# Top-k attention, a gated MLP and routed experts in one kernel: where three pieces of the expert weights' conversion stand beside the routing of the last tokens

## The chip, the cores and the metric

The kernel runs on one core of one Trainium2 chip. A core has TensorE (matrix products), VectorE, ScalarE and GpSimd (elementwise work and reductions) and SyncE, which here only issues transfers; in the profile they are PE, DVE, ACT, POOL and SP. Transfers of every issuer are carried by 16 DMA engines. Each engine runs its own list of instructions in order and waits for others by semaphores. The metric is the device time of one execution in microseconds (us); lower is better.

## What is computed

Three stages, each fed by the one ahead of it. The reference, cut to its core:

```python
scores = scale * np.matmul(q, k.transpose(0, 1, 3, 2))          # 2 x 8 heads, 576 x 576
kth = np.partition(scores, -32, axis=-1)[..., -32:-31]
attn = softmax(np.where(scores >= kth, scores, -1e9))
x = np.matmul(attn, v)                                          # 1152 tokens x 512
xn = x / np.sqrt(np.mean(x * x, -1) + 1e-6) * rms_g
y = (silu(xn @ w_gate) * (xn @ w_val)) @ w_out                  # 512 -> 1536 -> 512
logits = y @ r_gate                                             # 8 experts, each token goes to its best one
# each expert takes its first 288 tokens, in their order
h = np.maximum(np.einsum('ecd,edf->ecf', disp, w1), 0.0)        # 512 -> 1024
out[i] = gate_w[i] * np.einsum('ecf,efd->ecd', h, w2)[expert_idx[i], pos[i]]
```

## The kernel before, in words

The 1152 tokens are nine tiles of 128, t = 0 to 8. Attention runs by head pair and tile; behind it, interleaved by hand-written slots (`at`, `advance`), run `norm(t)`, `moe1(t)` (the dense MLP of a tile) and `dispatch(t)` (its routing). A scheduler replays the traced instructions on a timeline of its own and so sets each engine's list. A block written under `tc.issue_after(ins)` is put in the list of the engine of `ins` behind `ins`; on other engines it has no effect. It orders and adds no semaphore.

**The routing of a tile** (L486 to L570): TensorE transposes the MLP's output `yx` (L490), ScalarE copies it to `xu` (L492) and sums the squares (L497), TensorE makes the logits (L503, eight small matmuls), VectorE copies them (L506) and takes the maximum (L526), GpSimd negates it (L529), ScalarE takes the exponentials `ex` (L531). VectorE makes `key`, `k8` and the one-hot `oh` (L533, L536, L539). TensorE counts the tokens ahead (L542, L543; L541 in tile 8 alone). VectorE makes the position of each token (L547 to L555) and its `slot` (L563), and GpSimd scatters the rows to `disp` in DRAM (L565). The MLP of the last tiles stands beside this: `hT` transposed by TensorE (L436) and copied (L422, L423), the product with `w_out` (L475) and `yx` (L481).

**The weights of the experts** are 16 matrices of 2 MB, counted here by n, their place in the load order `ORDER` (n = 0, 1 are expert 0's up and down, 2, 3 expert 1's, and 4 expert 2's up). SP loads each in two halves (L718). `size` (L723) sums its squares (ScalarE L731, into a scratch `junk`; VectorE L734; TensorE L736 adds over partitions) and finds a power of two by six small VectorE operations (L737 to L742 and the helpers L139, L142). `convert` (L749) writes the fp16 high part `hi` (L756 on ScalarE, L758 on VectorE) and the low part `lo` (L761 on VectorE). Raw matrices 2 and 3 have a buffer each; 4 is loaded into that of 2 when 2 has been split, and 5 into that of 3.

**The experts.** Expert 0 runs in two parts. Part "a" is its first 128 rows: the ones that tiles 0 to 7 have filled, so the gather "a" (a transposing DMA on ScalarE's queue, `xgT`, L772) and its `notes` (L785) are traced in tile 8's routing and wait for tile 7's scatter. Part "b" is the rest, 48 rows, gathered behind tile 8's scatter by GpSimd (`xb`, L828) and turned by SP (`xbT`, L832). The products (L845) are 96 matmuls each: up a, down a, up b, down b, up 1, then up e and down e - 1 for e = 2 to 7. An up product is evicted to `hE` (ScalarE L855, VectorE L856), a down product to `yT2` (L864); `send` transposes that (L883), scales it to `ob` (L885) and scatters it to the output (L887). Between them `ready()` (L904) does the `size` of matrix n + 1, the `convert` of n and the load of a later one, from n = 4 on.

The lines around the change are those behind the dense MLP, where `size` and `convert` of the first matrices are traced. In the kernel before, matrix 3 stands under `tc.issue_after(scat[-1].ins)`, an instruction of GpSimd, on which neither `size` nor `convert` has any instruction.

Of the kernel before, what the change touches and what calls it, by code (L numbers as in the profile page):

```python
# [1 line left out]

# [12 lines left out]
AF = mybir.ActivationFunctionType  # L15
OP = mybir.AluOpType
# [9 lines left out]
NT = N // P  # L26
# [19 lines left out]
def tile_topk_attention__then__moe__then__moe_routed(  # L46
# [3 lines left out]
    nc = tc.nc  # L50
# [79 lines left out]
    def pow2_below_rsqrt(out, back, x, by, t):  # L130

        nc.gpsimd.tensor_scalar(t[:, 0:1], x, by, TINY, op0=OP.mult, op1=OP.add)
        nc.gpsimd.tensor_tensor(t[:, 1:2], t[:, 0:1], mhalf, op=OP.pow)
        yield
        exponent(out, t[:, 1:2])
        invert(back, out)

    def exponent(out, x):
        nc.vector.tensor_scalar(out.bitcast(I32), x.bitcast(I32), 0x7f800000, None, op0=OP.bitwise_and)  # L139

    def invert(out, x):
        nc.vector.tensor_scalar(out.bitcast(I32), x.bitcast(I32), -1, 0x7f000000, op0=OP.mult, op1=OP.add)  # L142
# [338 lines left out]
        nc.scalar.activation(yx[t], yps, AF.Copy, scale=ydec)  # L481
        yield

    scat = []

    def dispatch(t):  # L486
        y = yx.pop(t)
# [10 lines left out]
        size = iter(()) if t == NT - 1 else pow2_below_rsqrt(yn[:, 1:2], yn[:, 2:3], yn[:, 0:1], 1.01, yn[:, 3:5])  # L498
# [6 lines left out]
        lg = route.tile([P, E], F32, name="lg")  # L505
# [22 lines left out]
        nm = route.tile([P, 4], F32, name="nm")  # L528
        nc.gpsimd.tensor_scalar(nm[:, 0:1], m8[:, 0:1], -1.0, None, op0=OP.mult)  # L529
        ex = route.tile([P, E], F32, name="ex", bufs=1)  # L530
        nc.scalar.activation(ex, lg, AF.Exp, bias=nm[:, 0:1], accum_out=nm[:, 1:2])  # L531
        key = route.tile([P, E], F32, name="key", bufs=1)
        nc.vector.scalar_tensor_tensor(key, lg, m8[:, 0:1], rank8, op0=OP.is_ge, op1=OP.mult)  # L533
        yield
# [10 lines left out]
        pos = route.tile([P, 4], F32, name="pos")  # L545
# [14 lines left out]
            gather("a", 0, 0, WA, ew, nc.scalar)  # L560
            notes("a", 0, 0, WA, ew, nc.scalar)
        slot = route.tile([P, 1], I32, name="slot")
        nc.vector.tensor_tensor(slot, pos[:, 3:4], pos[:, 2:3], op=OP.add)  # L563
        nc.gpsimd.tensor_tensor(cum, cum, oh, op=OP.add)
        scat.append(nc.gpsimd.indirect_dma_start(  # L565
            out=disp, out_offset=bass.IndirectOffsetOnAxis(ap=slot[:, :1], axis=0),
# [73 lines left out]
    for p in range(NP):  # L640
        t, hp = divmod(p, 4)
# [12 lines left out]
    for t in range(NT):  # L654
        ew = nc.vector if t in (0, 8) else nc.gpsimd
        t0 = (4 * t + 5) * SL
        at(t0 + 1, ahead(norm(t, ew), 300), 1)
        at(t0 + (12 if t < NT - 1 else 18), ahead(moe1(t, ew), 0), 2.7)
        at(t0 + 10 + 4 * SL, ahead(dispatch(t), 0), 3 if t < NT - 1 else 1)
    live = []  # L660
    slot = 0
# [30 lines left out]
    ORDER = [0, 1, 2, 3, 4]  # L692
# [9 lines left out]
    def place(j):  # L702
        x = slots[slot_of[j]].bitcast(F16)
        return x[:, :8 * DM], x[:, 8 * DM:]

    def raw_of(n):

        if n < 2:
            return slots[2 + n]
        return raws[n % 2 if n < 4 else n % 4]  # L710
# [12 lines left out]
    def size(j, n):  # L723

        e, w = divmod(j, 2)
        raw = raw_of(n)
        sc = ew.tile([P, 13], F32, name="sc", bufs=8)
        k = 4 if n < 4 else 2
        for g in range(k):
            junk = ew.tile([P, BIG], BF16, name="junk")[:, :2 * BIG // k]  # L730
            nc.scalar.activation(junk, raw[:, g * 2 * BIG // k:(g + 1) * 2 * BIG // k], AF.Square, accum_out=sc[:, 9 + g:10 + g])  # L731
        t = pst.tile([P, DM], F32, name="st")
        s16 = ew.tile([P, 4], BF16, name="s16", bufs=2)
        nc.vector.tensor_copy(s16[:, :k], sc[:, 9:9 + k])  # L734
        for g in range(k):
            nc.tensor.matmul(t[:, 0:1], ones16, s16[:, g:g + 1], start=(g == 0), stop=(g == k - 1))  # L736
        nc.vector.tensor_scalar(sc[:, 2:3], t[:, 0:1], 1.01, TINY, op0=OP.mult, op1=OP.add)  # L737
        half_bits = sc[:, 3:4].bitcast(I32)
        nc.vector.tensor_scalar(half_bits, sc[:, 2:3].bitcast(I32), 1, 0x7fff0000, op0=OP.logical_shift_right, op1=OP.bitwise_and)
        nc.vector.tensor_scalar(half_bits, half_bits, -1, 0x5f370000 + ((10, 14)[w] << 23), op0=OP.mult, op1=OP.add)  # L740
        exponent(sc[:, 7:8], sc[:, 3:4])
        invert(sc[:, 4:5], sc[:, 7:8])  # L742
        if w == 0:
            es[e] = sc
        else:
            nc.vector.tensor_tensor(es[e][:, 8:9], es[e][:, 4:5], sc[:, 4:5], op=OP.mult)
        sized[j] = sc

    def convert(j, n):  # L749

        raw, (hi, lo), sc = raw_of(n), place(j), sized.pop(j)
        k = 4 if n < 4 else 2
        for g in range(k):
            r = slice(g * 2 * BIG // k, (g + 1) * 2 * BIG // k)
            if 2 * g < k:
                nc.scalar.activation(hi[:, r], raw[:, r], AF.Copy, scale=sc[:, 7:8])  # L756
            else:
                nc.vector.tensor_scalar(hi[:, r], raw[:, r], sc[:, 7:8], None, op0=OP.mult)  # L758
        for g in range(k):
            r = slice(g * 2 * BIG // k, (g + 1) * 2 * BIG // k)  # L760
            nc.vector.scalar_tensor_tensor(lo[:, r], raw[:, r], sc[:, 7:8], hi[:, r], op0=OP.mult, op1=OP.subtract)  # L761
# [31 lines left out]
    def fetch_w():  # L793
        n = loaded[0]
        loaded[0] += 1
        if n < 2 * E:
            load(ORDER[n], n)
# [11 lines left out]
    convert(0, 0)  # L809
    size(2, 2)  # L810
    convert(1, 1)
    convert(2, 2)
    fetch_w()
    with tc.issue_after(scat[-1].ins):
        size(3, 3)
        convert(3, 3)
    pacc = ctx.enter_context(tc.tile_pool(name="pacc", bufs=3, space=PSUM, reuse_waits="tile"))
    pback = ctx.enter_context(tc.tile_pool(name="pback", bufs=2, space=PSUM, reuse_waits="tile"))
# [85 lines left out]
    def ready():  # L904

        n = done[0]
        done[0] += 1
        if n >= 2 * E:
            return
        if n == 4:  # L910
            size(ORDER[4], 4)
        if n + 1 < 2 * E:
            size(ORDER[n + 1], n + 1)
        convert(ORDER[n], n)
        fetch_w()

    down("a", 0, WA)
    up("b", 0, WB)
    ready()
    send("a", WA, True)  # L920
    up(1, 1, W)
    ready()
    down("b", 0, WB)
    ready()
    cnt = pback.tile([P, DM], F32, name="back")
    nc.tensor.matmul(cnt[:, :E], ones16, cum, start=True, stop=True)
# [82 lines left out]
```

## Time and profile before

| | |
|---|---|
| three timed runs | 710.47, 708.5, 710.53 us; median 710.47 |
| the profiled execution | 708.96 us, of which the span of the trace is 707.2 |
| busy, share of the span | TensorE 79%, its weight loads 57%, VectorE 89%, ScalarE 70%, GpSimd 59% |
| chain that ended last | VectorE 49%, issue 16%, TensorE 11%, ScalarE 8%, DMA 8%, GpSimd 6% |
| mean granted TensorE clock | 0.935 |

VectorE searches the top 32 of attention up to 497 us; the last product of the dense MLP ends at about 558 us (L475 of tile 8, from 555.50 for 2.33), and the experts follow to the end of the span. A row of a timeline gives start, duration, engine, line, operation, what it writes and reads, and in brackets how long the engine stood idle just before and what released it. The chain is a backward walk from the last instruction. In a row with xN, N instructions lie behind one another and the duration is that of all. The clock is a share of full speed.

### The profile page before, as it was taken

How to read it: one execution, taken by the hardware profiler on the slowest of the kernel's cores; microseconds unless marked ns; L12 is line 12 of the kernel's file. 1: busy time of each engine (PE TensorE's matmuls, PEld its weight loads, DVE VectorE, ACT ScalarE, POOL GpSimd, SP SyncE). 2: the span in 40 equal slices, each digit the busy share in tenths (PEclk: the TensorE clock that was granted, in tenths of full speed). 3: DMA queues.
4: the chain of work that ended last, by engine and by line, in shares of the span. 5: the costliest groups of instructions: out<-in, count | busy, mean ns of one | idle time of the engine just before them, and what ended most of it. 6: DMA issues, size and time to landing. Idle time of an engine off the chain costs nothing.

```text
span 707.2 us, 13015 instructions
## 1 busy us (share of the span) xinstructions
PE 555.5 (79%) x4708; PEld 401.9 (57%) x4708; DVE 627.0 (89%) x1311; ACT 495.8 (70%) x959; POOL 414.9 (59%) x444
## 2 busy tenths in 40 slices
PE   1207424567667999999999999998999489989995
PEld 1106324435344666666656666664645289989994
DVE  3999999999999999999999999999348855999960
ACT  3446537558957879868878797876799537988921
POOL 2786887877696887966767778566631110022312
PEclk9999555679999999999999999999999889999998
DMA  8898171375000001000000000000570449999201
GB/s 244 236 331 282 39 233 38 126 225 188 15 8 8 16 31 43 16 31 10 16 23 16 24 16 24 1 1 16 205 286 1 148 82 382 328 322 347 106 21 38
DMA packets 47016, 80.00 MB, mean 113 GB/s; under 512 B 18732, under 2 KB 23340, under 8 KB 46946
## 3 DMA queue, kind: packets, MB, share of 16 engines
q1 hardware_dynamic: 43954, 74.02, 33.2%
q0 software_dynamic: 1792, 4.83, 1.9%
q8 instruction: 39, 0.64, 0.4%
q10 hardware_dynamic: 1200, 0.26, 0.2%
q14 instruction: 31, 0.25, 0.1%
HBM read 64.35 MB, written 12.27 MB: 108 GB/s over the span
## 4 chain that ended last, share of the span: by engine, by line
DVE 49%; issue 16%; PE 11%; ACT 8%; DMA 8%; POOL 6%; SPq 1%; POOLq 0%; ACTq 0%; DVEq 0%
DVE r L333 14%; DVE m L336 14%; DVE m L324 5%; PE pm L450 4%; DMA wbig<-in_w_out_dram 3%; DVE wbig L157 3%; ACT junk L731 3%; DMA raw<-in_w_dram 3%; POOL out_dram L887 2%; DVE wbig L159 2%; DVE split L761 2%; DVE wbig L228 2%; DMA vt<-in_v_l_dram 2%; PE pm L475 2%; DVE hT L423 1%
## 5 line engine op out<-in xcount | busy, mean ns | idle before, releaser
L450 PE MATMUL pm<-wbig,xn 128*128 128x512 f16 x600 | 152.1, 387 | 8.8 <-POOL wbig L225 3.2
L336 DVE MAX8 m<-r 128x8 f32<-128x576 f32 x216 | 156.8, 745 | 0.3
L845 PEld LDWEIGHTS <-split 128*128 128x128 f16 x1728 | 115.6, 99 | 6.9 <-DMA xbT<-xb 2.5
L310 PE MATMUL tp<-kst,qh 128*128 128x288 f32 (+1 forms) x160 | 65.2, 418 | 63.5 <-ACT s L312 24.2
L353 POOL TENSOR_TENSOR pp<-s,pp 128x576 f32<-128x576 f32 x72 | 102.8, 1442 | 8.6 <-ACT pp L352 8.4
L333 DVE MATCH_REPLACE8 r<-m,r 128x576 f32<-128x576 f32 x144 | 106.3, 740 | 0.0
L450 PEld LDWEIGHTS <-xn 128*128 128x128 f16 x648 | 62.4, 100 | 71.9 <-issue 11.3
L475 PE MATMUL pm<-wbig,hT 128*128 128x512 f16 x324 | 79.1, 383 | 7.7 <-POOL wbig L229 3.7
L310 PEld LDWEIGHTS tp<-kst,qh 128*128 128x128 f32 (+1 forms) x160 | 32.6, 205 | 89.9 <-ACT s L312 32.7
L376 PE MATMUL tp<-ident,pp 128*128 128x128 f32 x324 | 58.7, 298 | 16.1 <-ACT pp L358 7.5
L352 ACT ACTIVATE pp<-s,bias 128x576 f32<-128x576 f32 x72 | 52.0, 773 | 26.4 <-POOL bias L338 26.2
L312 ACT ACTIVATE s<-tp 128x288 f32<-128x288 f32 x144 | 54.8, 412 | 19.2 <-POOL pp L353 15.8
L761 DVE SCALAR_TENSOR_TENSOR split<-raw,sc,split 128x2048 f16<-128x2048 f32 (+1 forms) x32 | 65.8, 2078 | 0.1
L887 POOL DMA_INDIRECT out_dram<-ob,tos x14 | 20.2, 1445 | 73.8 <-ACT ob L885 58.4
L845 PE MATMUL acc<-hE,split 128*128 128x168 f16 (+2 forms) x864 | 58.8, 228 | 3.4 <-ACT junk L731 1.4
L731 ACT ACTIVATE junk<-raw 128x2048 bf16<-128x2048 f32 (+1 forms) x32 | 54.2, 1693 | 9.9 <-DMA raw<-in_w_dram 9.5
L384 PE MATMUL xps<-pt,vt 128*64 128x128 f32 (+1 forms) x800 | 57.8, 284 | 2.9 <-ACT pt L377 2.9
L376 PEld LDWEIGHTS tp<-ident,pp 128*128 128x128 f32 x324 | 42.5, 152 | 31.0 <-ACT pp L358 10.3
L377 ACT ACTIVATE pt<-tp 128x384 f32<-128x384 f32 x108 | 49.3, 494 | 14.9 <-PE tp L376 12.3
L845 PE MATMUL acc<-xgT,split 128*128 128x168 f16 (+1 forms) x768 | 58.0, 239 | 0.0
L358 ACT ACTIVATE pp<-pp,bias 128x576 f32<-128x576 f32 x72 | 56.4, 785 | 0.1
L324 DVE MAX8 m<-s 128x8 f32<-128x576 f32 x72 | 53.6, 745 | 0.0
(198 smaller groups left out, 1233.4 us busy)
## 6 DMA issues: line engine op xcount, KB each, us to landing
raw<-in_w_dram SPq DMA_DIRECT2D x28, 1024.0 KB, 10.2
wbig<-in_w_out_dram SPq DMA_DIRECT2D x6, 1024.0 KB, 8.1
disp<-wraw SPq DMA_DIRECT2D x18, 257.0 KB, 5.5
qraw<-in_q_l_dram SPq DMA_DIRECT2D x72, 64.0 KB, 2.2
wraw<-in_w_gate_dram SPq DMA_DIRECT2D x8, 512.0 KB, 4.5
split<-in_w_dram SPq DMA_DIRECT2D x4, 1024.0 KB, 5.8
kraw<-in_k_l_dram SPq DMA_DIRECT2D x12, 288.0 KB, 4.4
wbig<-in_w_val_dram SPq DMA_DIRECT2D x3, 1024.0 KB, 7.4
```

The source lines that it names most:

```text
L310: nc.tensor.matmul(sp[:c1], x[:, i, :c1], kst[b, hp][:, i, c * HALF:(c + 1) * HALF], start=(n == 0), stop=(n == 1))
L324: nc.vector.max(m[:, i, 0], s[i])
L333: nc.vector.match_replace(r[i], m[:, i, n - 1], src, -3.0e38)
L336: nc.vector.max(m[:, i, n], r[i])
L353: nc.gpsimd.tensor_tensor(w, s[i], w, op=OP.subtract)
L376: nc.tensor.transpose(tp[:, i, :], p2[:, o:o + P], ident)
L384: nc.tensor.matmul(xps[t][rows, hp, c0:c1], v, w, start=(n == 0), stop=(n == 4))
L450: nc.tensor.matmul(a, xn[:, x + c, :], half(i, lo), start=(c == 0 and n == 0), stop=(c == KC - 1 and n == 2))
L475: nc.tensor.matmul(yps, hT[f // KC][:, KC * hi + f % KC, :], half(i, lo), start=(f == 0 and n == 0), stop=(f == NF1 - 1 and n == 2))
L731: nc.scalar.activation(junk, raw[:, g * 2 * BIG // k:(g + 1) * 2 * BIG // k], AF.Square, accum_out=sc[:, 9 + g:10 + g])
L761: nc.vector.scalar_tensor_tensor(lo[:, r], raw[:, r], sc[:, 7:8], hi[:, r], op0=OP.mult, op1=OP.subtract)
L845: nc.tensor.matmul(a, u[:, c, col * P:(col + 1) * P], v[:, c, :a.shape[-1]], start=(c == 0 and n == 0), stop=(c == nk - 1 and n == 2))
```

## The change

Three pieces are put elsewhere, and no arithmetic changes. `dispatch` keeps the instruction `ex` (ScalarE) and `slot` (VectorE) of each tile, and a helper `after(t, ...)` opens `issue_after` on the ones named. The split of matrix 2 now stands behind those of tile 7 (NT - 2), the split of matrix 3 behind those of tile 8 (NT - 1), while the sizing of 3 stands free; the squares of matrix 4 stand behind `ex` of tile 8 on ScalarE.

```diff
--- before.py
+++ after.py
@@ -1,4 +1,4 @@
-from contextlib import ExitStack
+from contextlib import ExitStack, contextmanager
 
 import concourse.bass as bass
 import concourse.tile as tile
@@ -481,7 +481,15 @@
         nc.scalar.activation(yx[t], yps, AF.Copy, scale=ydec)
         yield
 
-    scat = []
+    scat, behind = [], {}
+
+    @contextmanager
+    def after(t, *engines):
+
+        with ExitStack() as stack:
+            for e in engines:
+                stack.enter_context(tc.issue_after(behind[t, e].ins))
+            yield
 
     def dispatch(t):
         y = yx.pop(t)
@@ -528,7 +536,7 @@
         nm = route.tile([P, 4], F32, name="nm")
         nc.gpsimd.tensor_scalar(nm[:, 0:1], m8[:, 0:1], -1.0, None, op0=OP.mult)
         ex = route.tile([P, E], F32, name="ex", bufs=1)
-        nc.scalar.activation(ex, lg, AF.Exp, bias=nm[:, 0:1], accum_out=nm[:, 1:2])
+        behind[t, "act"] = nc.scalar.activation(ex, lg, AF.Exp, bias=nm[:, 0:1], accum_out=nm[:, 1:2])
         key = route.tile([P, E], F32, name="key", bufs=1)
         nc.vector.scalar_tensor_tensor(key, lg, m8[:, 0:1], rank8, op0=OP.is_ge, op1=OP.mult)
         yield
@@ -560,7 +568,7 @@
             gather("a", 0, 0, WA, ew, nc.scalar)
             notes("a", 0, 0, WA, ew, nc.scalar)
         slot = route.tile([P, 1], I32, name="slot")
-        nc.vector.tensor_tensor(slot, pos[:, 3:4], pos[:, 2:3], op=OP.add)
+        behind[t, "dve"] = nc.vector.tensor_tensor(slot, pos[:, 3:4], pos[:, 2:3], op=OP.add)
         nc.gpsimd.tensor_tensor(cum, cum, oh, op=OP.add)
         scat.append(nc.gpsimd.indirect_dma_start(
             out=disp, out_offset=bass.IndirectOffsetOnAxis(ap=slot[:, :1], axis=0),
@@ -809,10 +817,11 @@
     convert(0, 0)
     size(2, 2)
     convert(1, 1)
-    convert(2, 2)
+    with after(NT - 2, "act", "dve"):
+        convert(2, 2)
     fetch_w()
-    with tc.issue_after(scat[-1].ins):
-        size(3, 3)
+    size(3, 3)
+    with after(NT - 1, "act", "dve"):
         convert(3, 3)
     pacc = ctx.enter_context(tc.tile_pool(name="pacc", bufs=3, space=PSUM, reuse_waits="tile"))
     pback = ctx.enter_context(tc.tile_pool(name="pback", bufs=2, space=PSUM, reuse_waits="tile"))
@@ -908,7 +917,8 @@
         if n >= 2 * E:
             return
         if n == 4:
-            size(ORDER[4], 4)
+            with after(NT - 1, "act"):
+                size(ORDER[4], 4)
         if n + 1 < 2 * E:
             size(ORDER[n + 1], n + 1)
         convert(ORDER[n], n)
```

All lines from L484 on are 8 further down in the new file (L563 becomes L571), those from about L845 on 9.

On VectorE, at tile 7's routing, the kernel before has this order (`split_5636` is matrix 2, `split_5637` matrix 3):

```order
L758 TENSOR_SCALAR split_5636<-raw_5638,sc 128x1024
L533 SCALAR_TENSOR_TENSOR key<-lg,m_5661,rank_72 128x8
L758 TENSOR_SCALAR split_5636<-raw_5638,sc 128x1024
L737 TENSOR_SCALAR sc<-st 128x1
L761 SCALAR_TENSOR_TENSOR split_5636<-raw_5638,sc,split_5636 128x1024
L536 MAX k_5684<-key 128x8
L761 SCALAR_TENSOR_TENSOR split_5636<-raw_5638,sc,split_5636 128x1024 x2
L739 TENSOR_SCALAR sc<-sc 128x1
L761 SCALAR_TENSOR_TENSOR split_5636<-raw_5638,sc,split_5636 128x1024
L548 TENSOR_SCALAR nm<-nm 128x1
L539 TENSOR_SCALAR oh<-rank_72,k_5684 128x8
L423 TENSOR_TENSOR hT<-pm,hT 128x512
```

The kernel after has, from the position's last steps to the first instruction of tile 8's chain:

```order
L558 SCALAR_TENSOR_TENSOR scr,pos<-px,oh 128x8
L561 TENSOR_SCALAR pos<-pos 128x1
L562 TENSOR_TENSOR pos<-pos 128x1
L571 TENSOR_TENSOR slot<-pos 128x1
L766 TENSOR_SCALAR split_5636<-raw_5638,sc 128x1024
L423 TENSOR_TENSOR hT<-pm,hT 128x512
L766 TENSOR_SCALAR split_5636<-raw_5638,sc 128x1024
L769 SCALAR_TENSOR_TENSOR split_5636<-raw_5638,sc,split_5636 128x1024 x4
L881 CAST to_6405<-notes_5889 128x1
L518 TENSOR_SCALAR yn<-yn 128x1
```

The six large operations of matrix 2 moved from between the steps of tile 7's routing to behind its slot; those of matrix 3 are no longer in this stretch. Tile 8's slot is followed by them.

On ScalarE, at the routing of tile 8, before (`junk,sc<-raw_5638` are the squares of matrix 4):

```order
L422 ACTIVATE hT<-pm 128x512
L756 ACTIVATE split_5637<-raw_5639,sc 128x1024 x2
L481 ACTIVATE yx<-pm,st 128x512
L731 ACTIVATE junk,sc<-raw_5638 128x2048
L492 ACTIVATE xu<-px 128x512
L772 DMA_TRANSPOSE xgT<-disp 128x8x128
L785 DMA notes_5889<-disp 128x2
L497 ACTIVATE yd,yn<-yx 128x512
L731 ACTIVATE junk,sc<-raw_5638 128x2048
L518 ACTIVATE yd<-yx,yn 128x512
L531 ACTIVATE ex,nm<-lg,nm 128x8
```

and after:

```order
L422 ACTIVATE hT<-pm 128x512
L780 DMA_TRANSPOSE xgT<-disp 128x8x128
L481 ACTIVATE yx<-pm,st 128x512
L793 DMA notes_5889<-disp 128x2
L505 ACTIVATE yd,yn<-yx 128x512
L500 ACTIVATE xu<-px 128x512
L526 ACTIVATE yd<-yx,yn 128x512
L539 ACTIVATE ex,nm<-lg,nm 128x8
L764 ACTIVATE split_5637<-raw_5639,sc 128x1024 x2
L864 ACTIVATE hE_6036<-acc 128x512
```

The squares of 4 and the split of 3 left the stretch ahead of `ex`, and the gather "a" moved ahead of `yx`. Further on, both squares of matrix 5 now stand ahead of the eviction of up b and of the split of 4, where they stood behind them.

On TensorE, at the sum of the squares of matrix 5 (`s_6383`), before:

```order
L845 LDWEIGHTS split_5635
L845 MATMUL acc<-hE_6262,split_5635 128x48
L736 LDWEIGHTS ones_70
L736 MATMUL st<-s_6383,ones_70 128x1
L736 LDWEIGHTS ones_70
L736 MATMUL st<-s_6383,ones_70 128x1
L845 LDWEIGHTS split_5635
L845 MATMUL acc<-hE_6261,split_5635 128x48
```

and after:

```order
L854 LDWEIGHTS split_5636
L854 MATMUL acc<-xgT,split_5636 128x168
L744 LDWEIGHTS ones_70
L744 MATMUL st<-s_6383,ones_70 128x1
L744 LDWEIGHTS ones_70
L744 MATMUL st<-s_6383,ones_70 128x1
L854 LDWEIGHTS split_5636
L854 MATMUL acc<-xgT,split_5636 128x168
```

The sum moved from behind the first 8 matmuls of down b to the middle of up 1, with 49 of its matmuls and all of down b behind it. Ahead of that, in tile 8's routing, L503 stood ahead of every product of up a; now 33 of them stand ahead of it, 25 more ahead of L541, 28 more ahead of L542, and 10 behind. Before, 22 stood between L503 and L541, 9 more ahead of L542, and 65 behind. In tile 7's, L542 and L543 stood behind the first two L475 and now stand ahead of them.

## Rows read from the trace of the kernel before

**Rows 1.** Timeline of VectorE around the routing of tiles 6 (508 us), 7 (548 us) and 8 (to 570.15).

```profile
508.00 0.17 DVE L526 MAX8 m<-lg 128x8 f32<-128x8 f32 x1
...
508.67 0.23 DVE L539 TENSOR_SCALAR oh<-rank,k 128x8 bf16<-128x8 f32 x1
...
547.95 0.17 DVE L526 MAX8 m<-lg 128x8 f32<-128x8 f32 x1
...
554.63 0.22 DVE L539 TENSOR_SCALAR oh<-rank,k 128x8 bf16<-128x8 f32 x1
...
556.03 1.41 DVE L758 TENSOR_SCALAR split<-raw,sc 128x1024 f16<-128x1024 f32 x2
557.35 0.15 DVE L563 TENSOR_TENSOR slot<-pos 128x1 int32<-128x1 f32 x1
...
557.49 4.87 DVE L761 SCALAR_TENSOR_TENSOR split<-raw,sc,split 128x1024 f16<-128x1024 f32 x4
...
570.15 0.15 DVE L563 TENSOR_TENSOR slot<-pos 128x1 int32<-128x1 f32 x1
```

**Rows 2.** Timeline of GpSimd, 558 to 575 us: the scatters of tiles 7 and 8 (L565) and the first instruction behind each that waited for its landing (L495 and L828).

```profile
558.30 1.43 POOL L565 DMA_INDIRECT disp<-yd,slot  x1 [2.92 <-DVE sc L746]
562.60 0.18 POOL L495 COPY yd<-tok 128x1 f32<-128x1 f32 x1 [2.86 <-DMA disp<-yd,slot]
...
571.17 1.06 POOL L565 DMA_INDIRECT disp<-yd,slot  x1 [1.19 <-DVE slot L563]
574.26 0.97 POOL L828 DMA_INDIRECT xb<-disp,rest  x1 [2.03 <-DMA disp<-yd,slot]
```

**Rows 3.** Timeline of ScalarE, 557 to 593 us; ACTq is its queue issuing a transfer.

```profile
557.93 0.67 ACT L481 ACTIVATE yx<-pm,st 128x512 f32<-128x512 f32 x1
...
562.56 1.36 ACTq L772 DMA_TRANSPOSE xgT<-disp  x1
...
563.76 0.58 ACT L492 ACTIVATE xu<-px 128x512 f32<-128x512 f32 x1
...
588.14 1.91 ACT L731 ACTIVATE junk<-raw 128x2048 bf16<-128x2048 f32 x1 [2.60 <-DMA raw<-in_w_dram]
...
591.63 1.91 ACT L731 ACTIVATE junk<-raw 128x2048 bf16<-128x2048 f32 x1 [0.43 <-DMA raw<-in_w_dram]
```

**Rows 4.** Timeline of TensorE, 545 to 603 us, and its four longest waits behind that.

```profile
545.48 0.95 PE L503 MATMUL px<-rg,xu 128*128 128x8 f32 x8
...
551.14 0.60 PE L436 MATMUL pm<-ident,gs 128*128 128x128 f32 x4
...
555.50 2.33 PE L475 MATMUL pm<-wbig,hT 128*128 128x512 f16 x10 [0.41 <-DVE sc L740]
...
564.39 1.88 PE L503 MATMUL px<-rg,xu 128*128 128x8 f32 x8 [5.08 <-ACT xu L492]
566.12 2.51 PE L845 MATMUL acc<-xgT,split 128*128 128x128 f16 x22
...
569.40 0.21 PE L542 MATMUL px<-oh,before 128*128 128x8 bf16 x1
...
575.33 4.79 PE L845 MATMUL acc<-hE,split 128*128 128x128 f16 x83 [0.51 <-DVE hE L856]
582.43 2.60 PE L845 MATMUL acc<-xbT,split 128*128 128x48 f16 x96 [2.30 <-DMA xbT<-xb]
...
593.89 0.19 PE L736 MATMUL st<-s,ones 128*128 128x1 bf16 x2 [1.27 <-DVE s L734]
593.94 2.38 PE L845 MATMUL acc<-hE,split 128*128 128x48 f16 x88
...
596.19 7.12 PE L845 MATMUL acc<-xgT,split 128*128 128x168 f16 x96
...
620.12 2.19 PE L845 MATMUL acc<-hE,split 128*128 128x168 f16 x28 [1.43 <-ACT junk L731]
...
636.26 1.47 PE L845 MATMUL acc<-hE,split 128*128 128x168 f16 x18 [1.09 <-ACT hE L855]
...
667.04 0.19 PE L736 MATMUL st<-s,ones 128*128 128x1 bf16 x2 [0.69 <-DVE s L734]
667.62 7.12 PE L845 MATMUL acc<-hE,split 128*128 128x168 f16 x96 [0.39 <-DVE hE L856]
```

**Rows 5.** The chain of waits in order of time, 545 to 600 us: start, duration, what.

```profile
554.68 7.15 DMA raw<-in_w_dram
...
566.26 2.36 PE acc L845 x22
...
583.51 10.72 DMA raw<-in_w_dram
```

**Rows 6.** Busy time by stretch: the stretch and its length; busy time and (count) of TensorE, its weight loads, VectorE, ScalarE and GpSimd; TensorE's granted clock; the DMA share; GB/s.

```profile
553.00:560.00 7.00, 3.21 (x17) 1.41 (x15) 7.00 (x24) 2.76 (x3) 1.64 (x2) 1.00 0.74 259
560.00:561.00 1.00, 0.00 (x0) 0.00 (x0) 1.00 (x1) 0.00 (x0) 0.00 (x0) 0.80 0.98 398
561.00:570.00 9.00, 5.61 (x48) 5.61 (x49) 4.78 (x26) 6.09 (x10) 0.64 (x3) 0.50 0.20 49
570.00:571.00 1.00, 1.00 (x13) 1.00 (x12) 0.30 (x4) 0.00 (x0) 0.00 (x0) 0.58 0.02 8
603.00:660.00 57.00, 54.49 (x745) 53.71 (x743) 53.69 (x90) 51.09 (x55) 13.02 (x7) 1.00 1.07 325
```

## The prediction

> **What bounds the kernel now.** I read the chain of waits first, then each engine's timeline where the dense MLP ends and the routed experts begin (547 to 604 us), then the clock and the DMA share there. Three things are to be seen.
>
> First, the routing of the last two token tiles is what the experts wait for, and for tile 7 it stands in a row with weight splits on VectorE. In tile 6 the one-hot `oh` starts 0.67 us after the maximum of the logits (508.00 to 508.67); in tile 7 it takes 6.68 us (547.95 to 554.63), and the slot comes at 557.35 [rows 1]. The scatter of tile 7 is issued at 558.30, GpSimd sees it landed at 562.60, and the gather of the first 128 rows (`xgT` "a", L772 on ScalarE's queue) starts at 562.56 [rows 2, 3].
>
> Second, ScalarE's squares of matrix 4 wait for a load that takes 7.15 us from 554.68, and `xu` of tile 8 stands behind these squares and the gather, at 563.76; TensorE waits 5.08 us for it and only then runs tile 8's logits (L503) and the first expert's products [rows 3 to 5]. In the 9 us from 561 TensorE's granted clock is 0.50 of full, its level of 1.2 GHz; it is 0.58 in the next and 1.00, 2.4 GHz, in the later ones [rows 6].
>
> Third, behind tile 8's slot (570.15) the chain goes on through its scatter (571.17), the gather of the rest (574.26) and the load of matrix 5 (from 583.51); ScalarE squares the halves of 5 at 588.14 and 591.63, and TensorE stops 1.27 us, to 593.89, for the sum of these squares [rows 1 to 5]. From 603 to 660 VectorE is busy 53.7 of 57 us, ScalarE 51.1, TensorE 54.5, and the DMA share is full [rows 6]. What is late at 603 has little room to be made up.
>
> **Tile 7's routing (gain).** With the splits of matrix 2 behind the slot, `oh` comes 0.67 after 547.95, plus some small operations: about 548.7. The position matmuls (L542, L543) stand behind four transposes L436, which end at 551.14 + 0.60 = 551.74 [rows 4]; they, not VectorE, now set the position, and the slot follows at about 552.3 (0.75 us from L542 to the slot in tile 8, 569.40 to 570.15 [rows 1, 4], less what runs together). That is 5.0 us before 557.35. The scatter was issued 0.95 after the slot's start in tile 7 and 1.02 in tile 8, and was seen landed 4.30 and 3.09 us later (558.30 to 562.60; 571.17 to 574.26) [rows 1, 2]. Landing after: 552.3 + 0.9 + 3.1 to 4.3, 556.3 to 557.5. I take 556.3: the load of matrix 4, beside which the longer one ran [rows 5], can't start before the splits of 2 have read its buffer, at about 557. The landing comes 6.3 us earlier.
>
> **ScalarE (mixed).** Its order now has the gather "a" ahead of `yx` (L481). `yx` could start at about 556.1, when the last ten L475 (2.33 us [rows 4]) end, behind `hT` at 553.8 (the slot, 0.15, one L758 of 0.7 [rows 1], and a last step about as long), but the engine waits for tile 7's landing and issues for 1.36 us [rows 3]: `yx` at 557.7 against 557.93. Some 1.6 us of a possible 1.8 are given up. But the squares of 4 no longer stand ahead of `xu`: `yx` takes 0.67 us, the notes' issue and L497 I put at as much each, and `xu` comes at 559.7 against 563.76 [rows 3].
>
> The gather lands at most 3.6 us after its issue starts (562.56, to the first products at 566.12 to 566.26 [rows 3, 5]): 556.3 + 3.6 = 559.9. It ran beside little; now the load of 4 begins a microsecond behind it. The nearest row for that is the scatter, 1.2 us longer beside a load, the upper bound; the lower one is below nothing by a little, since 3.6 also holds TensorE's own wait for L503. I take nothing: most of the gather lies ahead of the load.
>
> The Trainium skill, "DMA: Bandwidth & Descriptors", section "Issuing engines are not separate DMA queues", says that transfers issued by ScalarE, SP or GpSimd end on the same 16 engines and interleave. It speaks against the change, which moves the load of 4 from beside the scatter to beside the gather. The two scatters agree, 4.30 us beside the load and 3.09 without. By that rule tile 8's slot would come up to 1.2 us later than in my sum; the sum doesn't use it.
>
> **TensorE up to tile 8's slot.** The new order puts 33 of the first expert's products, which need the gather, ahead of L503, and 53 more between L503 and the position matmuls (31 before). A product takes 2.36/22 = 0.107 us at 1.2 GHz [rows 5] and 4.79/83 = 0.058 at 2.4; the eight L503 take 1.88 and 0.95 [rows 4]. From 559.9:
>
> At full clock: 33 x 0.058 + 0.95 + 53 x 0.058 + 0.75 = 6.7, slot at 566.6, 3.55 us earlier than 570.15. With a fall as now, the full clock back some 6.4 us after TensorE resumed (564.39, to between 570 and 571 [rows 4, 6]): 33 x 0.107 + 1.88 = 5.4, nine products more at 0.107, 44 at 0.058, 0.75: slot at 569.6, 0.55 earlier. At 1.2 GHz all the way: 3.5 + 1.88 + 5.7 + 0.75 = 11.8, 571.7, 1.6 later.
>
> Which? Before the clock fell, at 560 to 561, TensorE had been busy 3.21 us of the 7 from 553 on, and then stood [rows 6]. After the change the stretch looks much the same: L436 to 551.7, L475 from 553.8 to 556.1, four L490 (0.66 us), then a wait of some 0.8 us for the gather. I take the middle case: the work ahead is as thin, only the last wait is shorter.
>
> **Behind tile 8 (loss).** The splits of matrix 3 (1.41 us of `hi` and 4.87 of `lo` [rows 1] on VectorE, as much `hi` on ScalarE) move behind tile 8's slot and `ex`. They cost nothing: VectorE is busy only 5.1 of the 10 us from 561 to 571 [rows 6], and the first product that reads them, down 1, stands behind up 1 and up 2. The squares of 4 go behind that too. On SP's queue the gathers of 1, of the rest and of 2 and 3 still stand ahead of the load of 5, so this load moves with tile 8's landing, and with it the squares of its second half and their sum on TensorE.
>
> But TensorE's own order changes at this sum. Before, it stood inside the rest's second product ("down b") with 88 matmuls behind it: 2.38 us until up 2 could start [rows 4]. Now 49 of up 1 and all 96 of down b stand behind it: 49 x 7.12/96 = 3.63 and 96 x 2.38/88 = 2.60, together 6.23. Up 2 starts 3.85 us later, measured from the sum. Next late would be the splits of 4, which ScalarE now runs behind both squares of 5: `hi` 2 us from about 595, then `lo` on VectorE, ready at about 599, ahead of up 2 at 600. Nothing is added; with that cover gone, it would be a microsecond or two.
>
> After 603 TensorE's present stalls of 1.43, 1.09, 0.69 and 0.39 us [rows 4] may go: 3.6 at the most. New ones may come: the sum of 6 now stands 20 matmuls into up 2, and down b's evictions lie nearer to up 3. By the same rows I give these 1 to 1.4 us each, 2.4 at the most, an estimate. Bounds -3.6 to +2.4; I take 0, since the same engines are as full.
>
> **Sum.** -0.55 + 3.85 = +3.3 us. The profiled run took 708.96 us, of which 707.2 are the span; what lies outside stays. So 712.3 on that run. The three timed runs (710.47, 708.5, 710.53) have their median 1.5 above it; on the middle of the two, 709.7, it is 713.0.
>
> **Rivals.** Rival 1, no change: TensorE keeps its full clock through the routing of tile 8. For it: the wait ahead of the products shrinks from 5.08 to 0.8 us. Against: the work ahead is as thin. Then the slot's 3.55 pay for the 3.85: +0.3, 710.0.
>
> Rival 2, faster: full clock, and the later stalls go too, since the squares stand further ahead of the evictions that TensorE waited for (1.43 behind squares, 1.09 behind `hE` [rows 4]). -3.55 + 3.85 - 3.6 = -3.3: 706.4. Against: ScalarE has 6 us free in those 57, and the same squares must run there.
>
> Rival 3, slower still, by a second fall of the clock. Before, TensorE waited 2.30 us for the rest ahead of up b [rows 4]. Of the products "a" 10 instead of 65 now stand behind the position matmuls, so the wait grows by 55 x 0.058 = 3.2, to 5.5. If the clock falls there and comes back after 6.4 us again, half of that is lost: 3.2 on top of 3.3, 716.2. It decides from a wait about as long as the 5.08 us ahead of L503.
>
> **How the numbers follow.** Forecast 0.50, rival 1 0.27, rival 2 0.13, rival 3 0.10. The range 708.0 to 716.5 leaves out rival 2's middle and the ends of the others. About 0.3% (2 us) is what a measurement of this kernel can tell from no change. Slower: 0.45 of the forecast's cases and 0.09 of rival 3's, 0.54. Same: 0.25 of rival 1, 0.05 of the forecast, 0.01 of rival 3, 0.31. Faster: rival 2 and 0.02 of rival 1, 0.15.
>
> **What would show it.** Tile 7's slot near 552.3, the gather "a" issued near 556.3, `xu` of tile 8 near 559.7; the granted clock from 561 to 566 at 0.50 (forecast) or 1.00 (rivals 1 and 2); tile 8's slot near 569.6 or 566.6; up 2 starting near 599.5; TensorE's stalls after 603 of 3 to 5 us in all. The prediction is wrong if up 2 starts before 598, or if those stalls differ by more than 3 us from before.

## The result, and the profile after

The changed kernel takes 720.86 us in the median (718.21 to 721.27, four runs), the kernel before 710.5: a ratio of 1.0148, 95% interval 1.0116 to 1.0179. It is slower by 10.4 us, where the prediction's sum was 3.3 (713.0), and lies above the range of 708.0 to 716.5. The profiled execution is the fastest of the four, 718.21 us, span 716.3. Two executions far off the rest, of e9 (1421.12 us) and of the kernel before beside e9 to e12 (796.71), are left out of all times below.

In that execution tile 7's maximum comes at 548.41, 0.46 later than in [rows 1], ahead of what the change moves (it lies between 545.6 and 549.7 in all profiles); stages are therefore counted from this maximum. TensorE's timeline:

```profile
563.35 3.68 PE L854 MATMUL acc<-xgT,split 128*128 128x128 f16 x33 [3.81 <-DMA xgT<-disp]
566.82 1.42 PE L511 MATMUL px<-rg,xu 128*128 128x8 f32 x8
...
576.31 1.44 PE L854 MATMUL acc<-hE,split 128*128 128x128 f16 x12 [4.05 <-DVE hE L865]
579.30 7.38 PE L854 MATMUL acc<-hE,split 128*128 128x128 f16 x83 [1.55 <-DVE hE L865]
586.51 2.58 PE L854 MATMUL acc<-xbT,split 128*128 128x48 f16 x96
...
596.29 0.19 PE L744 MATMUL st<-s,ones 128*128 128x1 bf16 x2 [3.26 <-DVE s L742]
596.35 3.71 PE L854 MATMUL acc<-xgT,split 128*128 128x168 f16 x49
...
602.30 2.60 PE L854 MATMUL acc<-hE,split 128*128 128x48 f16 x96 [2.23 <-DVE hE L865]
604.74 1.61 PE L854 MATMUL acc<-xgT,split 128*128 128x168 f16 x20
```

Against [rows 4], the waits of 5.08 us ahead of L503 and of 2.30 ahead of up b are gone. In their place stand 3.81 us for the gather, 4.05 and 1.55 at the start of down a for evictions (5.6 in all), 3.26 at the sum of 5 (1.27 before) and 2.23 ahead of down b. VectorE:

```profile
552.75 0.16 DVE L571 TENSOR_TENSOR slot<-pos 128x1 int32<-128x1 f32 x1
...
571.79 0.15 DVE L571 TENSOR_TENSOR slot<-pos 128x1 int32<-128x1 f32 x1
571.86 1.41 DVE L766 TENSOR_SCALAR split<-raw,sc 128x1024 f16<-128x1024 f32 x2
573.18 2.48 DVE L769 SCALAR_TENSOR_TENSOR split<-raw,sc,split 128x1024 f16<-128x1024 f32 x2
575.58 0.68 DVE L865 SCALAR_TENSOR_TENSOR hE<-acc,hE 128x512 f16<-128x512 f32 x1
576.18 2.47 DVE L769 SCALAR_TENSOR_TENSOR split<-raw,sc,split 128x1024 f16<-128x1024 f32 x2
578.57 0.68 DVE L865 SCALAR_TENSOR_TENSOR hE<-acc,hE 128x512 f16<-128x512 f32 x1
...
596.92 2.34 DVE L769 SCALAR_TENSOR_TENSOR split<-raw,sc,split 128x2048 f16<-128x2048 f32 x1
...
599.25 2.34 DVE L769 SCALAR_TENSOR_TENSOR split<-raw,sc,split 128x2048 f16<-128x2048 f32 x1
...
601.57 0.67 DVE L865 SCALAR_TENSOR_TENSOR hE<-acc,hE 128x504 f16<-128x504 f32 x1
```

Tile 7's slot is where it was forecast. Behind tile 8's slot the splits of 3 run, and the evictions of up a (L865), for which TensorE stands, start behind them. Later the `lo` of 4 stands ahead of up 1's eviction (601.57), whose accumulator down b needs. ScalarE:

```profile
556.74 1.36 ACTq L780 DMA_TRANSPOSE xgT<-disp  x1
...
559.58 0.60 ACT L500 ACTIVATE xu<-px 128x512 f32<-128x512 f32 x1
...
590.68 1.91 ACT L739 ACTIVATE junk<-raw 128x2048 bf16<-128x2048 f32 x1 [14.42 <-DMA raw<-in_w_dram]
...
594.03 1.91 ACT L739 ACTIVATE junk<-raw 128x2048 bf16<-128x2048 f32 x1 [1.34 <-DMA raw<-in_w_dram]
...
595.94 0.47 ACT L864 ACTIVATE hE<-acc 128x384 f16<-128x384 f32 x1
596.31 0.68 ACT L894 ACTIVATE ob<-back,notes 128x512 f32<-128x512 f32 x1
596.88 2.00 ACT L764 ACTIVATE split<-raw,sc 128x2048 f16<-128x2048 f32 x1
```

The gather, issued at 556.74, feeds its first product at 563.35, 6.6 us later; and from 576 to 594 ScalarE waits 14.42 + 1.34 us for the load of 5, with the eviction of up b (its products ended at 589.1) and the `hi` of 4 queued behind the squares. Busy time by stretch, with columns as in [rows 6] (the last three are TensorE's granted clock, the DMA share and GB/s):

```profile
561.00:563.00 2.00, 0.00 (x0) 0.00 (x0) 0.00 (x0) 0.00 (x0) 0.00 (x0) 0.50 1.11 297
...
568.00:572.00 4.00, 3.86 (x69) 3.74 (x69) 2.59 (x19) 2.96 (x6) 0.46 (x2) 1.00 0.00 2
572.00:576.00 4.00, 0.22 (x1) 0.10 (x1) 4.00 (x5) 4.00 (x4) 1.39 (x1) 0.81 0.18 68
...
580.00:583.00 3.00, 3.00 (x31) 3.00 (x30) 0.14 (x1) 0.00 (x0) 0.00 (x0) 0.50 1.45 72
...
586.00:589.00 3.00, 3.00 (x112) 3.00 (x108) 0.75 (x1) 0.00 (x0) 0.00 (x0) 1.00 1.05 328
```

The granted clock falls twice, once as before and once in the waits of down a, whose last 83 products take 7.38 us instead of 4.79.

**Stages of all runs**, worked out from each profile: start of tile 7's maximum to tile 8's slot, from there to the first product of up b, to the first of up 2, to the end of the span; then the median, and that of the kernel before, timed beside it.

| | to slot 8 | to up b | to up 2 | to end | us | before |
|---|---|---|---|---|---|---|
| before | 22.2 | 12.3 | 13.8 | 111.0 | 710.5 | |
| the change | 23.4 | 14.7 | 18.2 | 111.6 | 720.9 | 710.5 |
| e1 split 2 only | 28.1 | 12.1 | 13.6 | 111.0 | 714.8 | 710.9 |
| e2 split 3 only | 22.6 | 13.8 | 19.4 | 112.9 | 718.5 | 710.9 |
| e3 squares 4 only | 22.2 | 12.8 | 14.2 | 111.2 | 712.5 | 710.9 |
| e4 load 4 held | 18.0 | 14.2 | 19.1 | 111.1 | 714.2 | 710.9 |
| e5 squares 5 late | 25.1 | 14.1 | 13.5 | 116.2 | 718.5 | 710.2 |
| e6 split 3 behind up a | 23.4 | 11.9 | 13.8 | 111.0 | 710.6 | 710.2 |
| e7 = e4 + e5 | 19.0 | 14.1 | 12.9 | 118.0 | 714.6 | 710.2 |
| e8 = e4 + e5 + e6 | 19.0 | 12.9 | 15.2 | 112.9 | 708.7 | 710.2 |
| e9 e6, order of 5 put back | 25.7 | 11.6 | 20.5 | 112.3 | 721.0 | 710.9 |
| e10 sum of 5 late only | 23.2 | 14.7 | 20.2 | 118.2 | 728.2 | 710.9 |
| e11 two loads early | 21.2 | 15.3 | 14.5 | 109.7 | 709.7 | 710.9 |
| e12 e11, squares 5 late | 18.2 | 15.7 | 13.1 | 114.2 | 713.6 | 710.9 |
| e13 before, order of 5 | 22.3 | 12.9 | 18.0 | 109.8 | 714.0 | 711.2 |
| e14 = e4 + e6 | 21.5 | 13.0 | 15.4 | 110.8 | 708.6 | 711.2 |

The change loses 1.2 + 2.4 + 4.4 + 0.6 = 8.6 us in its profile. A row is one execution, and differences of some 2 us in a stage tell little: e8 and e14 have the same lists, and their first stage takes 19.0 and 21.5 us, since the clock was back at 1.00 by 564 in one and by 568 in the other; the change and e5 have the same lists up to the slot, with 23.4 and 25.1.

### The profile page after: what moved, and what is told of

It reads as the page before. It is cut to its first block, busy times and chain, and to the rows that moved or that the text cites. A ratio compares the mean times of both kernels' runs of the same rounds, so it can differ in the third digit from the quotient of the medians.

```text
span 716.3 us, 13014 instructions
## 1 busy us (share of the span) xinstructions
PE 558.7 (78%) x4708; PEld 405.4 (57%) x4708; DVE 627.3 (88%) x1311; ACT 495.8 (69%) x959; POOL 421.1 (59%) x444
## 4 chain that ended last, share of the span: by engine, by line
DVE 49%; issue 21%; PE 13%; POOL 7%; ACT 5%; DMA 3%; SPq 1%; POOLq 0%; ACTq 0%; DVEq 0%
DVE r L333 15%; DVE m L336 14%; DVE m L324 5%; PE pm L450 4%; DVE wbig L157 4%; POOL out_dram L896 3%; DVE wbig L159 3%; PE pm L475 2%; DVE wbig L228 2%; DMA wbig<-in_w_out_dram 2%; PE late L450 1%; PE xps L384 1%; DVE hT L423 1%; POOL pp L353 1%; PE acc L854 1%
## 5 line engine op out<-in xcount | busy, mean ns | idle before, releaser
L854 PEld LDWEIGHTS <-split 128*128 128x128 f16 x1728 | 119.2, 101 | 16.1 <-issue 12.7
L475 PE MATMUL pm<-wbig,hT 128*128 128x512 f16 x324 | 79.1, 383 | 8.0 <-POOL wbig L229 3.7
L854 PE MATMUL acc<-hE,split 128*128 128x168 f16 (+2 forms) x864 | 62.0, 235 | 8.6 <-DVE hE L865 7.8
L739 ACT ACTIVATE junk<-raw 128x2048 bf16<-128x2048 f32 (+1 forms) x32 | 54.2, 1693 | 21.0 <-DMA raw<-in_w_dram 18.2
L312 ACT ACTIVATE s<-tp 128x288 f32<-128x288 f32 x144 | 54.8, 412 | 19.1 <-POOL pp L353 15.8
L896 POOL DMA_INDIRECT out_dram<-ob,tos x14 | 22.6, 1617 | 69.4 <-ACT ob L894 67.3
L376 PEld LDWEIGHTS tp<-ident,pp 128*128 128x128 f32 x324 | 42.5, 153 | 31.1 <-ACT pp L358 10.3
```

What stands on the lines that cost most here:

```text
L376: nc.tensor.transpose(tp[:, i, :], p2[:, o:o + P], ident)
L475: nc.tensor.matmul(yps, hT[f // KC][:, KC * hi + f % KC, :], half(i, lo), start=(f == 0 and n == 0), stop=(f == NF1 - 1 and n == 2))
L854: nc.tensor.matmul(a, u[:, c, col * P:(col + 1) * P], v[:, c, :a.shape[-1]], start=(c == 0 and n == 0), stop=(c == nk - 1 and n == 2))
```

## The experiments

**One part at a time.** e1, e2 and e3 each keep one of the three pieces of the change. The expectations weigh three readings of the loss, T, R1 and R2, which the first one gives.

```diff
 e1 keeps:  with after(NT - 2, "act", "dve"):  convert(2, 2)
 e2 keeps:  size(3, 3); with after(NT - 1, "act", "dve"):  convert(3, 3)
 e3 keeps:  with after(NT - 1, "act"):  size(ORDER[4], 4)
```

> Only the split of matrix 2 stands behind tile 7's slot; the split of 3 and the squares of 4 are as in the kernel before. Theory T (three terms make the loss: the load of 4 beside the gather a, 3.0 us; TensorE's sum of 5 ahead of up 1 and down b, 3.9 us; the eviction of up b behind the squares of 5 on ScalarE, 2.2 us): the split of 3 now takes the place of that of 2 ahead of tile 7's position, so its slot stays at about 557.5; the load of 4 starts later, near 564; 26 products stand ahead of L503 and wait for the gather, so tile 8's slot comes 3 to 4 us later than before; the sum of 5 has 63 matmuls behind it, 0.7 us less than before. About 713.5. Rival R1 (TensorE's clock is the loss): as slow as the change, 720, if the clock falls twice. Rival R2 (the split of 3 behind tile 8's slot is the loss, since the eviction of up a waits behind it and TensorE stands 5.6 us ahead of down a): no loss, 710.5.

> Only the split of matrix 3 stands behind tile 8's slot (with its sizing free). T: tile 7's slot 1.4 us earlier, tile 8's about as before, since its squares of 4 still wait for the load; the sum of 5 stands with 47 of up 1 and all of down b behind it, +3.7; the eviction of up b has one square of 5 ahead of it and no loss. About 713.5. R2: TensorE stands ahead of down a as in the change and nearly the whole loss is here, 718 to 721. R1: 712 if the clock is low once, 718 if it falls twice.

> Only the squares of matrix 4 stand behind tile 8's exponentials. T: xu of tile 8 no longer waits for the load and comes near 559.5, L503 runs ahead of every product, tile 8's slot some 0.7 us earlier than before (24 products at the low clock stand between, and need the gather, landed near 566); the sum of 5 has the 96 matmuls of down b behind it, +0.2. About 710. R1 and R2: 710.5, nothing lost either; this run tells whether this part gains anything by itself.

e1 measured 1.0070 (1.0043 to 1.0097), 714.8 us, all of it at tile 8's slot and near T's number; e2 1.0114 (1.0076 to 1.0151), nearly all behind the slot; e3 1.0016 (0.9987 to 1.0045), no difference. So the squares of 4 make no loss that shows by themselves. e2 met the number of R2 (also R1's for two falls of the clock) and not T's; where it lost (1.5 ahead of up b, 5.6 ahead of up 2, 1.9 behind) fits none alone.

**The load of 4 held.**

```diff
     with after(NT - 2, "act", "dve"):
         convert(2, 2)
-    fetch_w()
+    probe = dram.tile([P, 8], F16, name="probe")
+    landed = nc.sync.dma_start(probe, xgT["a"][:, 0, :8])
+    with tc.issue_after(landed.ins):
+        fetch_w()
```

> The whole change, with the load of matrix 4 held on SP until the gather a has landed (a scrap of the gathered rows is copied ahead of it). T: the gather takes 3.6 instead of 6.6 us, tile 8's slot comes 3 us earlier (near 568.5 in the time of the change's trace), everything behind it too: about 718. R1: no change if the clock is low there anyway, 721. R2: 721, since the split of 3 and the eviction stand where they stood.

714.16, ratio to the kernel before 1.0048 (1.0025 to 1.0071): 6.7 us less than the change, more than the 3 of T. The lists of VectorE, ScalarE and TensorE are those of the change, so the time of the load is all that differs. The gather feeds TensorE 3.25 us after its issue (556.58, on ScalarE's queue), the clock stays at 1.00 from 560 to 566, and the slot comes 5.4 us earlier in its stage. The clock's part of that isn't sure to come: in e14, with the load held too and a wait of 0.43 us for the gather, it was 0.50 from 562 to 566. The two waits behind are still there:

```profile
559.83 2.00 PE L857 MATMUL acc<-xgT,split 128*128 128x128 f16 x33 [0.45 <-DMA xgT<-disp]
...
570.75 1.11 PE L857 MATMUL acc<-hE,split 128*128 128x128 f16 x12 [4.05 <-DVE hE L868]
...
591.03 0.19 PE L744 MATMUL st<-s,ones 128*128 128x1 bf16 x2 [4.14 <-DVE s L742]
```

**The squares of 5, and the split of 3.**

```diff
 e5, in ready(), n == 4:
+            convert(ORDER[4], 4)
+            with after("b", "act"), after(4, "hi"):
+                size(ORDER[5], 5)
 e6:
-    with after(NT - 1, "act", "dve"):
-        convert(3, 3)
     up("a", 0, WA)
+    with after("a", "act", "dve"):
+        convert(3, 3)
```

> The whole change, with ScalarE's squares of matrix 5 queued behind the eviction of up b and behind the hi part of matrix 4. TensorE's sum of 5 then stands 18 matmuls into down b again, with 78 behind it (88 in the kernel before). The split of 3 stays ahead of the eviction of up a. T: TensorE runs up 1 without a stop to about 596.6 in the time of the change's trace, the sum of 5 is ready at 596.3, up 2 starts at 599.3 instead of 604.7: 5.4 us less than the change, about 715.5. R2 (the split of 3 ahead of the eviction of up a): no gain, 721. R1 (clock): the same second fall of the clock ahead of down a, so no gain, 720.

> The whole change, with the split of matrix 3 behind the evictions of up a on both engines instead of behind tile 8's slot and exponentials. The planner then also puts the squares of 5 behind the eviction of up b and TensorE's sum of 5 into down b, 68 matmuls behind it. T: as in the run with the squares of 5 moved, and a microsecond more, since TensorE no longer stands 5.6 us ahead of down a and reaches up b when its rows land: about 714.5. R2: the whole loss that the split of 3 makes goes, 712 to 715, while the run with the squares moved alone gains nothing. R1: the second fall of the clock goes with the wait, 3 us gained, 718.

> The load of 4 held until the gather a has landed, and the squares of 5 behind the eviction of up b and the hi part of 4 (the two runs put together). T: tile 8's slot near 566.2 as with the load held, up 1 without a stop, the sum of 5 at about 591 inside down b, up 2 near 593.3 instead of 599.5: some 6 us less than with the load held alone, about 708, 2.5 us faster than the kernel before. R2: 714, as with the load held alone. R1: 712 to 714.

> The load of 4 held, the split of 3 behind the evictions of up a, and the squares of 5 behind the eviction of up b and the hi part of 4. T: TensorE reaches up b when its rows land (near 578.5), but the sum of 5 still waits for its load, near 591; up 2 near 592.8: about 707.5. R2: 709 or less, with the gain over the load held alone all from the split of 3. R1: without the second fall of the clock some 3 us less than with the two put together, 705.

e5: 718.45, 1.0107 (1.0072 to 1.0142). Up 2 came 4.7 us sooner in its stage, as T had it, and the stretch behind gave 4.6 back. e7 the same: 714.55, 1.0049 (1.0016 to 1.0081), 6.2 gained and 6.9 given back over e4. So T's numbers (715.5 and 708) weren't met. What VectorE does there is seen in its groups by line from 600 to 700 us (busy, mean, then the idle time ahead of them and what ended it), e5 first and then e6:

```profile
L865 DVE SCALAR_TENSOR_TENSOR hE<-acc,hE 128x504 f16<-128x504 f32 (+1 forms) x19 | 11.1, 610 | 5.9 <-ACT hE L864 5.8
```

```profile
L863 DVE SCALAR_TENSOR_TENSOR hE<-acc,hE 128x504 f16<-128x504 f32 (+1 forms) x18 | 10.6, 616 | 0.9 <-ACT hE L862 0.8
```

The planner (the scheduler that sets each engine's list) had made another one for all that follows, in which VectorE waits 5.8 us for ScalarE's evictions. TensorE's own waits behind up 2 come to 7.1 us in e5 and 8.9 in e7, against 3.7 in e6 and 3.8 before. VectorE's waits alone don't make the loss: in e2 they come to 7.0 us in the same stretch, and its last stage is 1.9 longer than before. e6: 710.58, 0.9997 (0.9966 to 1.0028): the whole loss is gone. R1, the clock as the loss, had 718 here and falls: the clock is at 0.50 three times in this profile (560 to 564, 574 to 576, 584 to 586), and the run is as fast as the kernel before. But the planner also put the squares of 5 behind the eviction of up b there, and the sum into down b, so this run alone doesn't say which. e8: 708.65, 0.9962 (0.9921 to 1.0003), near the numbers of T (707.5) and R2 (709 or less).

**Which of the two.** e9 is e6 with the order around the sum of 5 put back by force; e10 moves TensorE's sum alone; e13 puts that order into the kernel before.

```diff
 e9 on e6, e13 on the kernel before (squares and sum of size() split):
+    squares(ORDER[5], 5)
     up("b", 0, WB)          # its eviction on ScalarE now behind them
 e9 also: the sum behind matmul 47 of up 1
 e10 on the change: the sum behind matmul 8 of down b
```

> As the run with the split of 3 behind the evictions of up a, but with the order around the sum of 5 forced as in the change: the sum stands 47 matmuls into up 1, and ScalarE's eviction of up b stands behind both squares of 5. T, as it now stands (TensorE's sum ahead of up 1 and down b, and the eviction behind the squares, cost by themselves): up 2 starts 4 to 6 us later than in that run, 715 to 716. R2 (all of the loss comes from the split of 3 ahead of the eviction of up a, the order of the sum only follows): no loss, 710.6.

> The whole change, with TensorE's sum of 5 alone put back to where the kernel before has it, 8 matmuls into down b; ScalarE's order around the squares of 5 stays as in the change, the split of 3 too. T: up 1 runs through, the eviction of up b comes behind the squares at 597, down b ends near 599.6, and up 2 waits for the split of 4 to 601.6, 3.1 us earlier than in the change: 717.8 in the end if what follows keeps its pace. R2: no gain, 721. A third reading, from the two runs with the squares moved, where up 2 came 4 to 6 us earlier and the rest took 5 to 7 us longer: up 2 near 601.6, but the stretch behind it longer than 113 us, 720.

> The kernel before with one thing of the change alone: ScalarE's eviction of up b queued behind both squares of matrix 5 (the squares wait for the load of 5). Splits of 2 and 3 and squares of 4 stand where the kernel before has them. The sum of 5 on TensorE goes 72 matmuls into up 1. T as it now stands (the eviction of up b behind squares that wait for a load is the larger part of the loss): the eviction ends at 594 instead of 585.6, up 1 stops for the accumulator or the sum, down b starts at 597 to 598, up 2 near 601 instead of 596.2, with a fall of the clock on top where TensorE stands for more than 4 us: 715 to 719. R2 (the split of 3 ahead of the eviction of up a): 710.5. R1 (clock alone, no order): 710.5 to 712.

e9: 720.95, 1.0106 (1.0067 to 1.0146), against e6's 710.58 and 0.9997, with the split of 3 behind up a's evictions and the same lists up to the squares of 5 in both: 1.1%, some 8 us, by the ratios. R2 as the sole cause falls. Of the 10.0 us between the two profiles, 2.3 lie at tile 8's slot, ahead of what was forced, where the low clock lasted longer in e9; 6.7 lie at up 2, the place in question. There its profile has the sum and the low clock behind the wait, 49 products in 6.39 us for 3.71:

```profile
598.67 0.19 PE L754 MATMUL st<-s,ones 128*128 128x1 bf16 x2 [4.01 <-DVE s L752]
598.73 6.39 PE L864 MATMUL acc<-xgT,split 128*128 128x168 f16 x49
```

e10: 728.15, 1.0253 (1.0215 to 1.0291), worse than the change, which no reading had. With the sum out of its way TensorE stops in up 1 none the less, behind 72 matmuls, for the accumulator that up b's eviction holds, and again ahead of down b:

```profile
595.71 2.87 PE L866 MATMUL acc<-xgT,split 128*128 128x168 f16 x24 [2.77 <-DVE hE L882]
...
600.82 0.48 PE L866 MATMUL acc<-hE,split 128*128 128x48 f16 x8 [2.23 <-DVE hE L882]
```

A later wait of 7.03 us (at 650.20, for an eviction, in another list of the planner's) adds to it. e13: 713.98, 1.0046 (1.0022 to 1.0069): that order costs 4.2 us at up 2 without any of the change's three pieces; 1.2 come back behind it. That is a microsecond below T's range, and above the numbers of R1 and R2.

**A better version.** e11 and e12 load 4 and 5 early, into the buffers of the dense MLP's weights (e12 with e5's edit); e14 is e4 and e6 together, and its order is that of e8.

```diff
 e11, e12:
-        return raws[n % 2 if n < 4 else n % 4]
+        return raws[n % 2 if n < 4 else (n + 2) % 4]
     (both loads issued behind the gather a has landed)
```

> The load of 4 held until the gather a has landed and the split of 3 behind the evictions of up a, and the loads of 4 and 5 both issued there, into the two buffers that the dense MLP's weights leave (6 and 7 take the buffers of 2 and 3). The sum of 5 then stands ahead of up b. T and R2 both: nothing of matrix 5 is waited for any more; up b at 578.5 to 580.5 in the time of the run with all three, up 1 and down b behind it without a stop, up 2 near 592.5 instead of 595.7: about 705.5. If the load of 5 beside tile 8's scatter and the gathers costs as much as the load of 4 did beside the gather a (3 us): 708.5.

> The same with the squares of 5 behind the eviction of up b and the hi part of 4; the sum of 5 then stands 75 matmuls into up 1. T: the load is long there, so the sum waits for the squares alone; up 2 near 593: about 706. R2: the same. If VectorE's order behind up 2 is what sets the end, as in the two runs with the squares moved, up 2 comes early and the rest takes 5 us longer: 711.

> The load of 4 held until the gather a has landed and the split of 3 behind the evictions of up a, no more: the planner's order comes out as in the run with all three, so its time should too, 706 to 709 where the kernel before takes 710.5; five rounds, to tell whether this version is faster than the kernel before.

e11: 709.71, 0.9991 (0.9969 to 1.0013), no gain: tile 8's scatter, issued at 568.83, now ran beside the load of 5, and the gather of the rest that waits for it was issued 6.0 us later (574.84), against 3.1 in [rows 2]; up b waited 5.84 us for the rest, and the gain went there. e12: 713.62, 1.0053 (1.0027 to 1.0079), slower than was expected (706 or 711), with 114.2 us behind up 2. e14: 708.57, 0.9964 (0.9940 to 0.9989), in twelve runs: faster than both kernels, by 2.6 and 12 us. So from the change (720.9), holding the load takes off 6.7 us (e4) and the split of 3 behind up a's evictions, with the order that the planner then makes, 5.6 more (e14). The parts don't add: that split alone takes off 10.3 (e6).

## Why the prediction was wrong, step by step

**Tile 7's routing: right.** Slot 552.75 (552.3 forecast), gather issued at 556.74 (556.3), `xu` at 559.58 (559.7).

**The gather beside the load: mis-sized.** I took nothing, upper bound 1.2 from the scatter. It took 6.6 us to the first product, and 3.25 with the load held (e4): 3.3 us by the load. It was 6.0 to 6.6 us in the five profiles of the change, e5, e6, e9 and e10, and 3.2 to 3.3 in the six with the load held. The rule of the Trainium skill that the sum didn't use ("DMA: Bandwidth & Descriptors", section "Issuing engines are not separate DMA queues") held, and the gather paid more than the scatter. The clock fell as forecast, but was back at 1.00 by 568, so that L503's eight products took 1.42 us instead of the 1.88 forecast, and none behind them was slow. That was luck: in e5, with the same lists, it came back after 570, and the slot a further 1.7 us later. e4 gained 2 us more at the slot than the gather alone, in an execution whose clock stayed.

**"They cost nothing": failed.** Of the splits of 3 I looked at VectorE's free time and at the product that reads them, not at what stands behind them in VectorE's and ScalarE's lists: the evictions of up a. TensorE stood 5.6 us at the start of down a, and the clock fell a second time, rival 3's mechanism a product earlier than it had it. Up b came 2.4 us later from the slot; in e6, with the order mended, 0.4 sooner than before. In the change's own trace up 2 doesn't seem to pay for it: TensorE stands 3.26 us behind it for the sum of 5, whose squares go by their load. Accordingly e9, without the waits of down a but with that sum, isn't clearly faster than the change (1.0106 and 1.0148, with intervals that overlap).

**The sum of 5: right as far as it went.** 3.71 + 2.60 = 6.3 us behind it, 6.23 forecast.

**"Nothing is added": failed.** I let only the splits of 4 come behind the squares of 5. The eviction of up b stood there too, waiting for the load, and the splits of 4, pushed back, stood ahead of up 1's evictions: 2.23 us ahead of down b. Counted by the sum of 5, the 8.0 us at up 2 are, to a tenth, 1.2 at the slot, 0.8 for a sum that comes later behind it, 3.9 for what stands behind the sum (3.85 forecast) and these 2.2. e9 and e6 show that the order around these squares decides some 8 us, part of it by the low clock behind the wait; e10 that moving the sum alone gains nothing; e13 that the order costs without the change too (0.5%, 4.2 us at up 2).

**Behind up 2: right.** 111.0 to 111.6 in the profiles, with 3.1 us of TensorE's waits where 3 to 5 were forecast. The other three executions are 2 to 3 us slower than the profiled one, at mean clocks of 0.918 to 0.922 for 0.930; which stretch is longer in them no trace shows.

What stays open: why the lists of e5 and e7 take 5 to 7 us longer behind up 2 than those of e6, e8 and e14. TensorE's waits there are shown, and make up the larger part; whether the place of the split of 3 or the planner's own timeline makes them wasn't separated. So what the split of 3 costs by its place alone isn't shown either, since every run that moved it also got other lists.

## What to carry to other kernels

When a large piece is moved behind a given instruction on an engine that runs its list in order, cost it by what is queued behind it there (evictions that free accumulators above all), not by the engine's free time nor by who reads the piece. A piece that waits for a transfer is a costly one to have ahead of an eviction: 14.42 us of waiting stood ahead of up b's here. And where a planner makes the order, a moved piece changes lists far from it: read the new lists to the end of the program, and time stages, since a gain at one stage can be given back in the next. Before reading a stage from one profile, see how far it moves between profiles of the same lists (2.5 us here).

## What the runs showed of the hardware

A transposing gather of 128 rows took 6.0 to 6.6 us from its issue to the first product beside a 2 MB load (five profiles) and 3.2 to 3.3 without (six). An indirect scatter of 128 rows was seen landed after 3.1 us alone, 4.3 beside one load ([rows 2]), and 6.0 (e11) and 7.1 (e12) beside another. The low clock outlasted the waits: in the change it was 0.50 from 561 to 567, with TensorE at work from 563.35, and again from 576 to past 583, where 83 products took 7.38 us for 4.79, 2.6 us beyond the waits themselves. A long wait wasn't needed for it: in e14 the clock was 0.50 from 562 to 566 behind a wait of 0.43 us, and in e12, behind one of 0.49, it stayed at 1.00. What decides between the two no run here shows.
